# One weight gradient computed transposed and turned later, in a one-core forward-and-backward transformer block

## The chip, the core and the metric

The kernel runs on one core of one Trainium2 chip. The core has TensorE (PE; its weight loads are listed as PEld), VectorE (DVE), ScalarE (ACT), GpSimd (POOL), SyncE (SP) and 16 DMA engines. The metric is the device time of one execution in microseconds: the median of repeated runs. A change is judged by the ratio of its median to the one before.

## The reference

One transformer block, forward and backward, S = 2048 tokens of D = 640, in bfloat16. The outputs are the block's result and the gradients of six inputs, among them the three weights of the gated MLP (F = 1728).

```python
h  = x + A(layernorm(x), wqkv, wo)          # linear attention, 32 heads of 20
h2 = h + B(layernorm(h), w1, w3, w2)        # gated MLP

def B(x, w1, w3, w2):                       # x: [2048, 640]
    gate = x @ w1                           # [2048, 1728]
    up   = x @ w3
    hh   = silu(gate) * up
    return hh @ w2                          # w2: [1728, 640]

out, vjp = jax.vjp(f, A_x, A_wqkv, A_wo, B_w1, B_w3, B_w2)
grads = vjp(grad_out)                       # w2's gradient: hh.T @ grad_out, [1728, 640]
```

## The kernel before

The kernel is written as one stream of instructions by hand: the order in the source is the order in each engine's queue, and a queue stands still while its first instruction waits. Tokens are cut into 16 tiles of 128 rows. Data that a later stage needs in another layout is stored to DRAM and loaded back, often through a transposing DMA (`dmaT`, always issued on SP except for a few on ACT). `dma` issues on SP, `A.dma_start` on ACT, `dmaG` on POOL.

The stages, in order of time:

1. Norm and projections (0 to about 75 us). `load_x` brings in tiles of x, `stat` and `p1_norm` normalize them (on ACT for even tiles past 8, else on DVE), a table `v_steps` says beside which tile each of these is issued (steps marked "A" come ahead of the q activations of that tile, "B" behind), `trickle` says behind which tile a weight is loaded, and `outs` where results are stored. Tiles 8 and up are transposed by DMA (L250). `m_part` and `kvT_block` form the products for linear attention.
2. The MLP's forward pass and the first half of its backward pass (about 75 to 340 us), in four chunks of 512 tokens and 14 blocks of 128 columns of F (`mlp`). `mlp_ghh` computes one block of grad_out @ w2.T some calls ahead of its use (`AHEAD` = 2; 8 blocks are done before the loop). The side work of a chunk prepares the next chunk's tiles: `f2_at`, then `f2_hn` (normalize and store hn), then `f2_ht` (transpose it, by DMA for tiles 4 and up). `r_steps` says behind which block loads and stores of the attention's r are issued. `o2_steps` makes the output product with w2 of the chunk before, whose rows are loaded in four pieces in the first chunk.
3. w2's gradient (L1097; 340.5 to 399.4 us). `load_hh` brings hh from DRAM, transposed, in blocks of 512 columns (`blk`) with the first block in two halves. For each of 13 blocks of 128 rows of the gradient, two groups of 16 products run over the token tiles, with hh as the stationary operand and 320 columns of grad_out as the moving one. ACT copies the two banks (L1100) and issues the store to `out_6`. The last 64 rows go through `gw2_tail` (L1083): pairs of products, each on half of the array. Between the blocks SP is given the next loads: the last block of hh, the transposed w1 and w3 (`load_w13`), and the first two pieces of the gate's gradients (`load_gg`).
4. Gradients through the MLP's input and the attention (399.4 to 699.5 us): `ghn` (L1142), `gr`, then products of the attention, `dkv`, `gxn` (L1515).
5. The gradients of w1 and w3 (L1346; 699.5 to 816.2 us): seven blocks of up to 496 columns, five jobs of 16 products in each. `load_block(i + 2)` is issued when block i is done, since `gb` has two buffers. Each job's result is copied by ACT and stored from ACT's queue.

The core of stage 3:

```python
for j in range(2):
    for t in range(ST):
        T.matmul(acc[:, j, 0:HD], lhsT=hb[b][:, t, i * P:(i + 1) * P], rhs=g2[:, t, j * HD:(j + 1) * HD], ...)
A.copy(out=ob[:].rearrange("p (j n) -> p j n", j=2), in_=acc[:, :, 0:HD])
A.dma_start(out=out_6[fc * P:(fc + 1) * P, :], in_=ob[:])
```

Of the kernel before, what the change touches and what calls it, by code (L numbers as in the profile page):

```python
# [9 lines left out]
P = 128  # L10
# [15 lines left out]
NG = 27  # L26
# [29 lines left out]
def kernel(  # L56
# [39 lines left out]
    w_d = dram.tile([D, D], BF16, name="w_d")  # L96
    kvT_d = dram.tile([D, D], BF16, name="kvT_d")
    dwoT_d = dram.tile([D, D], BF16, name="dwoT_d")
    hn_d = dram.tile([S, D], BF16, name="hn_d")
    hh_d = dram.tile([F, S], BF16, name="hh_d")  # L100
    gg_d = dram.tile([2 * F, S], BF16, name="gg_d")
# [80 lines left out]
    def load_wq(a, b):  # L182
        dma(out=wqkv[:, :, a * HD:b * HD], in_=wq_v[:, :, a * HD:b * HD])

    def load_x(a, b):
        dma(out=x_sb[:, a:b, :], in_=xS[:, a:b, :])
# [133 lines left out]
    def q_tile(t):  # L320
        q_home(t)
        phi(p1_mm(t, 0), pqs[t], t)
# [101 lines left out]
    def m_part(m, tiles, js=(0, 1)):  # L424
        if m not in macc:
            macc[m] = [ps.tile([P, 512], F32, name="macc", tag=("m", "tr")[m % 2], bufs=2) for _ in range(2)]
        for t, j in [(t, j) for t in tiles for j in js]:
            n = HD + (m < 2) * j
            T.matmul(macc[m][j][:, 0:n], lhsT=pk_all[:, t, m * P:(m + 1) * P],  # L429
                     rhs=x_ext[:, t, j * HD:j * HD + n], start=(t == 0), stop=(t == ST - 1))  # L430
# [12 lines left out]
    def kvT_block(m, acc):  # L443

        a, b = M_H[m]
        n = (b - a) * DH
        for c in range(DT):
            T.matmul(acc[:, 0:n], lhsT=wqkv[:, c, 2 * D + m * P:2 * D + (m + 1) * P],
                     rhs=mT[:, c, a * DH:b * DH], start=(c == 0), stop=(c == DT - 1))
        masked(bd, acc[:, 0:n], m)  # L450
# [7 lines left out]
    zero_pads()  # L458
    load_w2T(0, 2 * P)
    load_g2T(0)  # L460
    load_x(8, 12)
    load_w2T(2 * P, 4 * P)
    load_wq(0, 2)
    load_x(12, ST)
    def warm_up(n, warm):
        for _ in range(n):
            T.matmul(warm[:, 0:P], lhsT=ones[:], rhs=ones[:], start=True, stop=True, skip_group_check=True)
# [34 lines left out]
    def load_wo():  # L502
        dma(out=wo[:], in_=A_wo.rearrange("(c p) n -> p c n", p=P))

    trickle = {4: w13[0], 5: w13[1], 9: lambda: load_wq(4, 6), 12: w13[2], 14: w13[3]}

    R = None
    v_steps = {1: (R, ("N", 4)), 2: (("S", 5), R, ("N", 5)), 3: (("S", 6), R, ("N", 6), ("C", 0)),
               4: (("S", 7), R, ("N", 7), ("S", 8)), 5: (R, ("N", 8), ("S", 9)), 6: (R, ("N", 9), ("S", 10)),
               7: (("S", 11), R, R, ("A", 10), ("L", 11)), 8: (("S", 12), R, R, ("S", 13)),  # L510
               9: (("N", 13), R, ("S", 14), ("B", 12)), 10: (R, R, ("S", 15)), 11: (R, ("B", 14), ("L", 15))}
    V_OPS = {"S": stat, "N": p1_norm, "C": p1_scale}

    def xn_out(g, q):
# [4 lines left out]
        sl = slice(g * TPC, (g + 1) * TPC)  # L519
        dma(out=pk_v[:, sl, :], in_=pk_all[:, sl, :])  # L520

    outs = {7: ((xn_out, 0, dma),), 8: ((group_out, 0),), 12: ((group_out, 1), (xn_out, 1, dma)), 13: ((group_out, 2),)}

    QT = (6, 7, 9, 11)
    M0 = {7: (0, 1, 2), 8: (3, 4, 5)}
# [47 lines left out]
    def big():  # L573
        return ps.tile([P, 2, 512], F32, name="bigx", tag="big", bufs=2)[:, 0]
# [49 lines left out]
    r_prod(5)  # L624
    m_part(4, range(5))
    q_tile(8)
    kvT_block(1, big())
    r_row(4)
    r_prod(6)
    phi_rest()  # L630
    m_part(4, range(5, 11))
    q_tile(9)
    phi_rest()
    for j in range(2):
# [110 lines left out]
    def f2_hn(t):  # L745
        hn[t] = (pf.tile([P, D], BF16, name="hn", tag="pql", bufs=4) if t == 2 else
                 pf.tile([P, D], BF16, name="hn", tag="h2", bufs=2) if t == 3 else
                 pf.tile([P, D], BF16, name="hn") if t % 2 else w2[:, FT, :])
        ln2.norm(hn[t][:], x_sb[:, t, :], t)
        if t < 2:  # L750
            f2_ht(t)
        for n in ((), (0, 1))[t] if t < 2 else (t,):
            dma(out=hn_v[:, n, :], in_=hn[n][:])
# [23 lines left out]
    def mlp_ghh(n):  # L777
        if n < SC * FT:
            ghh_chunk(n, lambda: ps.tile([P, W], F32, name="mm", bufs=4))
# [3 lines left out]
    def mlp(c, fc, between):  # L783

        k, i = divmod(fc, 2)
        n = c * FT + fc
        if n >= FILL - AHEAD:
            mlp_ghh(n + AHEAD)
        gp = mm5(w1, fc, hnT[c])
        if i == 0:  # L790
            pair[k] = [ew(name) for name in NAMES]
        sig, s2, gate, up = pair[k]
        A.activation(sig[:, i, :], gp[:], AF.Sigmoid)  # L793
        A.activation(s2[:, i, :], gp[:], AF.Sigmoid, scale=-1.0)
        drain(1)
        between()
        drain(1)
        if fc < FT - 1:
            upp = mm5(w3, fc, hnT[c])
            A.copy(out=up[:, i, :], in_=upp[:])  # L800
        else:
            V.memset(up[FL:, i, :], 0.0)
            A.copy(out=up[:FL, i, :], in_=gp[FL:])
        A.copy(out=gate[:, i, :], in_=gp[:])  # L804
        if i == 1:
            mlp_pair(c, k, *pair.pop(k), ghh.pop(n // 2))
# [152 lines left out]
    def sides(c):  # L959
        side = ({}, {})  # L960
        for i in range(TPC):
            k0 = 3 * i - (i == TPC - 1) * (1 + (c == 1)) + (-2, 1, 0)[c]
            for k, pos, f in ((k0 + 2, 1, f2_at), (k0 + 3, 0, f2_hn), (k0 + 3, 1, f2_ht)):
                if c == 0 and f is f2_at:
                    if i == 0:
                        continue
                    f = f2_at0
                if k0 == -2 and f in (f2_at0, f2_hn, f2_ht):
                    k, pos = (k + 1, 0) if f is f2_at0 else (k + 1, pos)
                if k >= 0:  # L970
                    side[pos].setdefault(k, []).append((f, i))
        return side
# [8 lines left out]
    def r_end(t):  # L981
        r_scale(t)
        r_out(t)

    r_steps = [{0: ((load_x, 6, 8),), 1: ((r4_out, 0, 2),), 2: ((r_load, 8),), 3: ((load_w2T, 10 * P, F),), 4: ((r_load, 9), (r4_out, 2, 4)),
                5: ((r_store, 7, 8),),
                10: ((xn_out, 2, dmaG),), 12: ((r_load, 10),)},
               {0: ((r_den, 8), (load_x, 8, 12)), 1: ((r_end, 8), (r_load, 11), (xn_out, 3, dmaG)), 2: ((r_den, 9),), 3: ((r_end, 9), (r_load, 12)),
# [4 lines left out]
    for c in range(SC):  # L993
# [3 lines left out]

        def run_side(pos, fc):
            if c + 1 < SC:
                for f, i in sorted(sides[c][pos].get(fc, ()), key=lambda x: (x[0] is f2_ht, x[1])):  # L1000
                    f((c + 1) * TPC + i)

        for fc in range(FT):
# [34 lines left out]
    drain(1)  # L1038


    hb, blk = {}, [(0, 512), (512, 512), (1024, 512), (1536, 192)]

    def load_hh(b):
        f0, fw = blk[b]
        hb[b] = U2.tile([P, ST, 512], BF16, name="hb", tag="ABCA"[b])
        for a, n in ((0, 2 * P), (2 * P, 2 * P)) if b == 0 else ((0, fw),):
            dmaT(out=hb[b][:, :, a:a + n], in_=hh_d[f0 + a:f0 + a + n, :])

    load_hh(0)
    for _ in o2_steps(SC - 1, A.dma_start):  # L1050
# [21 lines left out]
    def load_gg(j, c0, c1, q=dma):  # L1072
        if c0 == 0:
            ggb[j] = ba.tile([P, NG, 2 * P], BF16, name="ggb", bufs=2)
        q(out=ggb[j][:, c0:c1, :],
            in_=gg_d[c0 * P:c1 * P, j * 2 * P:(j + 1) * 2 * P].rearrange("(c p) w -> p c w", p=P))

    def gw2_tail():

        gt = ps.tile([P, 2, 512], F32, name="gt", tag="gw", bufs=4)  # L1080
        for t in range(ST):
            for j in range(2):
                T.matmul(gt[j * FL:(j + 1) * FL, 0, 0:HD], lhsT=hb[3][:, t, P:P + FL],  # L1083
                         rhs=g2[:, t, j * HD:(j + 1) * HD], start=(t == 0), stop=(t == ST - 1))
        ob = br.tile([P, HD], BF16, name="gts")
        A.copy(out=ob[:], in_=gt[:, 0, 0:HD])
        for j in range(2):
            A.dma_start(out=out_6[F - FL:F, j * HD:(j + 1) * HD], in_=ob[j * FL:(j + 1) * FL, :])

    for fc in range(FT - 1):  # L1090
        b, i = divmod(fc, 4)
        if fc == FT - 2:
            gw2_tail()
        acc = ps.tile([P, 2, 512], F32, name="gw", bufs=4)
        for j in range(2):
            for t in range(ST):
                T.matmul(acc[:, j, 0:HD], lhsT=hb[b][:, t, i * P:(i + 1) * P], rhs=g2[:, t, j * HD:(j + 1) * HD],  # L1097
                         start=(t == 0), stop=(t == ST - 1))
        ob = br.tile([P, D], BF16, name="gw2o", bufs=2)
        A.copy(out=ob[:].rearrange("p (j n) -> p j n", j=2), in_=acc[:, :, 0:HD])  # L1100
        A.dma_start(out=out_6[fc * P:(fc + 1) * P, :], in_=ob[:])
        if fc == 3:
            load_hh(3)
        if fc == 5:
            load_w13()
        if fc == 8:
            load_gg(0, 0, NG)
        if fc == 11:
            load_gg(1, 0, NG)
    ps.release()  # L1110
    U2.release()

# [437 lines left out]
    njob = 8  # L1550
    dmaT(out=g_h[:, 0:DT, :], in_=dwoT_d[:, :])
    dma(out=out3S, in_=g_h[:, 0:DT, :])
    for i, (f0, f1) in enumerate(blocks):
        n = f1 - f0
        for m in range(DT):
            last = (i, m) == (len(blocks) - 1, DT - 1)
            for a, b in ((0, n - P), (n - P, n)) if last else ((0, n),):
                c = (a + b) // 2
                halves = ((a, c), (c, b)) if i * DT + m < 5 else ((a, b),)
                out = [(x + y - a, z + y - a, to) for y, w in halves for x, z, to in both_grads(m, f0 + y, f0 + w)]  # L1560
                grad_job(hnN, m, lambda t: gb[i][:, t, a:b], b - a, out, A.dma_start)
        load_block(i + 2)
    ps.release()
    ex.release()
    bv.release()
# [33 lines left out]
```

## Time and profile before

| what | us |
|---|---|
| median of 3 runs | 822.12 (821.39 to 822.13) |
| profiled execution | 820.91 |
| span of its trace, first to last instruction | 819.1 |
| PE busy | 814.1 (5420 matmuls) |
| DVE busy | 452.4 |
| ACT busy | 323.6 |
| POOL busy | 130.9 |

By stretch of the span (us), with the busy time of three engines and the mean busy share of the DMA engines, which can pass 1 since packets in flight overlap:

| stretch | PE | DVE | ACT | DMA |
|---|---|---|---|---|
| 0 to 100 | 98.1 | 80.6 | 68.9 | 0.90 |
| 100 to 340.5 | 240.4 | 192.2 | 150.1 | 0.74 |
| 340.5 to 399.4 (w2's gradient) | 58.9 | 0.5 | 8.7 | 1.19 |
| 399.4 to 544.7 | 145.3 | 98.5 | 29.6 | 0.64 |
| 544.7 to 625.6 | 80.9 | 42.2 | 17.1 | 0.91 |
| 625.6 to 699.5 | 73.9 | 35.7 | 27.4 | 0.84 |
| 699.5 to 819.1 (w1's and w3's gradients) | 116.6 | 2.7 | 21.7 | 0.65 |

The granted clock of PE is 1.00 in all of them. All times are of one profiled execution; times on the span's clock start at its first instruction. Matmuls are pipelined, so the listed duration of one (299 ns at 320 columns) is longer than the distance from one to the next.

### The profile page before, as it was taken

The numbers are of one execution on the slowest core, as the hardware profiler recorded it, in microseconds if no ns is written. First come the engines' busy times: TensorE is split into PE (matmuls) and PEld (weight loads), VectorE is DVE, ScalarE is ACT, GpSimd is POOL, SyncE is SP. The second block draws the span as 40 slices with busy tenths as digits, with TensorE's granted clock in tenths as the row PEclk, the third lists the DMA queues.
The fourth block names the chain that finished last, engine by engine and source line by source line (L and its number), as shares of the span: only waits on it lengthen the run. The fifth ranks groups of instructions, "written<-read, shape, count | busy, mean of one in ns | idle before, by whom it ended". The sixth has DMA issues, their size and how long they took to land.

```text
span 819.1 us, 13944 instructions
## 1 busy us (share of the span) xinstructions
PE 814.1 (99%) x5420; PEld 512.8 (63%) x5420; DVE 452.4 (55%) x973; ACT 323.6 (40%) x603; POOL 130.9 (16%) x193
## 2 busy tenths in 40 slices
PE   9999999999999999999999999999999999999998
PEld 6677544555555555777777777777777777544444
DVE  7859987998898566300057777772781544200000
ACT  7856688665565666011122212222212334211111
POOL 2233333333222212100001111110220000000000
PEclk9999999999999999999999999999999999999999
DMA  9899699796485556999977877259974997967751
GB/s 264 219 290 239 166 244 327 225 245 173 127 211 156 169 170 167 222 261 226 257 176 180 211 197 200 58 107 187 287 195 93 181 194 159 239 164 186 160 141 36
DMA packets 323873, 157.88 MB, mean 193 GB/s; under 512 B 242784, under 2 KB 317056, under 8 KB 323808
## 3 DMA queue, kind: packets, MB, share of 16 engines
q1 hardware_dynamic: 281040, 116.18, 61.6%
q0 software_dynamic: 7328, 24.48, 8.7%
q10 hardware_dynamic: 35440, 16.34, 7.7%
q8 instruction: 42, 0.69, 0.4%
q14 instruction: 23, 0.19, 0.1%
HBM read 47.09 MB, written 51.13 MB: 120 GB/s over the span
## 4 chain that ended last, share of the span: by engine, by line
PE 96%; DVE 2%; ACT 1%; issue 0%; DMA 0%; POOL 0%; ACTq 0%; DVEq 0%
PE mm L394 20%; PE job L1346 20%; PE ghn L1142 14%; PE gxn L1515 8%; PE gw L1097 7%; PE o L910 4%; PE o L856 3%; PE gwo L1230 3%; PE big L267 3%; PE gr L1199 3%; PE dkv L1452 3%; PE macc L429 2%; PE at L654 2%; PE mm L267 1%; PE dkv L1380 1%; DVE st L147 1%
## 5 line engine op out<-in xcount | busy, mean ns | idle before, releaser
L1346 PE MATMUL job<-gb,hnN 128*128 128x496 bf16 (+3 forms) x576 | 116.8, 366 | 0.0
L1142 PEld LDWEIGHTS <-ggb 128*128 128x128 bf16 x864 | 84.5, 98 | 32.8
L1346 PEld LDWEIGHTS <-hnN 128*128 128x128 bf16 x576 | 55.8, 98 | 61.0
L394 PE MATMUL mm<-pqT,w 128*128 128x512 bf16 x405 | 93.8, 379 | 0.1
L394 PEld LDWEIGHTS <-w 128*128 128x128 bf16 x540 | 52.5, 98 | 63.4 <-issue 1.4
L1350 ACT CAST obs<-job 128x496 bf16<-128x496 f32 (+4 forms) x56 | 28.5, 510 | 123.7 <-PE job L1346 120.9
L1142 PE MATMUL ghn<-w13a,ggb 128*128 128x320 bf16 x448 | 63.5, 299 | 0.0
L1157 DVE SCALAR_TENSOR_TENSOR wb<-gs,hnb 128x640 f32<-128x640 bf16 x16 | 13.2, 825 | 88.7 <-ACT gs L1154 88.7
L1142 PE MATMUL ghn<-w13b,ggb 128*128 128x320 bf16 x416 | 61.4, 299 | 0.0
L394 PE MATMUL mm<-g2T,w2T 128*128 128x512 bf16 x240 | 59.6, 379 | 0.0
L1097 PE MATMUL gw<-g,hb 128*128 128x320 bf16 x416 | 56.8, 299 | 0.0
L1207 POOL TENSOR_TENSOR sz<-Zb,g_h 128x640 f32<-128x640 bf16 x16 | 20.2, 1261 | 197.7 <-DVE g_h L1208 197.7
L1097 PEld LDWEIGHTS <-hb 128*128 128x128 bf16 x416 | 40.6, 98 | 16.0 <-issue 0.3
L419 ACT CAST ghh<-mm 128x512 bf16<-128x512 f32 x48 | 28.3, 589 | 47.7 <-PE mm L394 40.1
L793 ACT ACTIVATE sig<-mm 128x512 bf16<-128x512 f32 x56 | 33.9, 605 | 26.4 <-PE mm L394 21.1
L1154 ACT ACTIVATE gs<-ghn 128x640 bf16<-128x640 f32 x16 | 11.3, 704 | 78.8 <-PE ghn L1142 73.9
L394 PEld LDWEIGHTS <-w2T 128*128 128x128 bf16 x260 | 25.4, 98 | 23.4
L267 PEld LDWEIGHTS <-pqT 128*128 128x128 bf16 x320 | 30.7, 98 | 13.7 <-ACT pqT L259 1.5
L267 PE MATMUL big<-wqkv,pqT 128*128 128x320 bf16 x250 | 38.6, 299 | 0.6 <-ACT pqT L259 0.3
L1346 PEld LDWEIGHTS <-g 128*128 128x128 bf16 x320 | 31.0, 98 | 11.5
L829 DVE TENSOR_TENSOR gate<-gate,sig 128x1024 bf16<-128x1024 bf16 x28 | 19.3, 689 | 33.2 <-ACT gate L804 30.5
L910 PE MATMUL o<-w,hhT 128*128 128x320 bf16 x224 | 35.0, 299 | 0.0
(219 smaller groups left out, 1369.9 us busy)
## 6 DMA issues: line engine op xcount, KB each, us to landing
hh_d<-hhT SPq DMA_DIRECT2D x24, 256.0 KB, 2.7
gg_d<-gate POOLq DMA_DIRECT2D x24, 256.0 KB, 4.3
gg_d<-ghh POOLq DMA_DIRECT2D x24, 256.0 KB, 3.4
ggb<-gg_d SPq DMA_DIRECT2D x6, 896.0 KB, 5.4
ggb<-gg_d ACTq DMA_DIRECT2D x6, 832.0 KB, 5.7
ggb<-gg_d SPq DMA_DIRECT2D x2, 1728.0 KB, 12.7
x_sb<-in_A_x_dram SPq DMA_DIRECT2D x5, 640.0 KB, 5.9
pk_d<-pk_all SPq DMA_DIRECT2D x4, 640.0 KB, 6.6
```

The source lines that it names most:

```text
L267: T.matmul(acc, lhsT=pqT[:, c, t * P:(t + 1) * P], rhs=wqkv[:, c, n0:n0 + HD], start=(c == 0), stop=(c == DT - 1))
L394: T.matmul(acc[:], lhsT=w[:, c, fc * P:(fc + 1) * P], rhs=rhs[:, c, :], start=(c == 0), stop=(c == DT - 1))
L419: A.copy(out=ghh[n // 2][:, n % 2, :], in_=acc[:])
L793: A.activation(sig[:, i, :], gp[:], AF.Sigmoid)
L856: T.matmul(accs[i, j][:, 0:HD], lhsT=hhT[c][:, fc, i * P:(i + 1) * P], rhs=w2[:, fc, j * HD:(j + 1) * HD], start=(first and fc == 0), stop ...
L910: T.matmul(o2["ps"][:, 0:HD], lhsT=hhT[c][:, fc, i * P:(i + 1) * P], rhs=w2[:, fc, j * HD:(j + 1) * HD], start=(fc == 0), stop=(fc == FT - 1))
L1097: T.matmul(acc[:, j, 0:HD], lhsT=hb[b][:, t, i * P:(i + 1) * P], rhs=g2[:, t, j * HD:(j + 1) * HD], start=(t == 0), stop=(t == ST - 1))
L1142: T.matmul(acc[:, j, 0:HD], lhsT=ggb[t // 2][:, k, lo:lo + P], rhs=rhs[:, j * HD:(j + 1) * HD], start=(k == 0), stop=(k == NG - 1))
L1199: T.matmul(gr[t][:, j, 0:HD], lhsT=ghT[t][:, c, :], rhs=wT2[:, c, j * HD:(j + 1) * HD], start=(c == 0), stop=(c == DT - 1))
L1346: T.matmul(acc[:, 0:n], lhsT=lhs[:, t, m * P:(m + 1) * P], rhs=rhs(t), start=(t == 0), stop=(t == ST - 1))
L1350: A.copy(out=ob, in_=acc[:, 0:n])
L1515: T.matmul(acc[:, j, 0:HD], lhsT=g, rhs=wqT[:, k, j * HD:(j + 1) * HD], start=(k == 0), stop=(k == 14))
```

## The change

Stage 3 computes the gradient's transpose: grad_out is now the stationary operand (five blocks of 128 columns) and hh the moving one, in four blocks of 256, 448, 512 and 512 columns. That gives 20 pieces of 16 products, each into one PSUM bank of one of two sets of four (`gw0`, `gw1`). Each piece is copied by ACT and stored, as it is, to a new DRAM tile `gw2T_d`; pieces of 448 columns are padded to 512 by a POOL memset. In stage 5, SP loads the four blocks back through the transposing DMA into free parts of `g_h` (`gw2_turn`), one behind each of the first four blocks, and stores each one block later to `out_6` (`gw2_out`). The tail function is gone. `load_hh` makes one transfer a block, and the loads between the pieces are issued at other places in the loop.

The rest changes orders. In stage 1, x tiles 10 and 11 are loaded with 12 to 15 instead of with 8 and 9, half of w3 and a store of pk are issued behind later tiles, tile 14 is normalized ahead of q's activations, and the second `kvT_block` comes behind a part of `m_part`. In stage 2, `f2_ht` is called in `f2_hn`, ahead of the store of hn, for tiles 4 and up, two transfers in `r_steps` change places, and `mlp_ghh` skips one call at the start of the second chunk and then runs one block ahead instead of two. In stage 5, eight jobs instead of five store in two parts.

```diff
+    gw2T_d = dram.tile([D, 4 * 512], BF16, name="gw2T_d")
...
-    load_x(8, 12)
+    load_x(8, 10)
     load_w2T(2 * P, 4 * P)
     load_wq(0, 2)
-    load_x(12, ST)
+    load_x(10, ST)
...
-    trickle = {4: w13[0], 5: w13[1], 9: lambda: load_wq(4, 6), 12: w13[2], 14: w13[3]}
+    trickle = {4: w13[0], 7: w13[1], 9: lambda: load_wq(4, 6), 12: w13[2], 14: w13[3]}
...
-               9: (("N", 13), R, ("S", 14), ("B", 12)), 10: (R, R, ("S", 15)), 11: (R, ("B", 14), ("L", 15))}
+               9: (("N", 13), R, ("S", 14), ("B", 12)), 10: (R, R, ("S", 15)), 11: (R, ("A", 14), ("L", 15))}
...
-    outs = {7: ((xn_out, 0, dma),), 8: ((group_out, 0),), ...
+    outs = {7: ((xn_out, 0, dma),), 9: ((group_out, 0),), ...
...
     q_tile(8)
-    kvT_block(1, big())
...
     m_part(4, range(5, 11))
+    kvT_block(1, big())
     q_tile(9)
...
         ln2.norm(hn[t][:], x_sb[:, t, :], t)
-        if t < 2:
+        if t < 2 or t >= TPC:
             f2_ht(t)
...
-        if n >= FILL - AHEAD:
-            mlp_ghh(n + AHEAD)
+        if FILL - AHEAD <= n < FT or n > FT:
+            mlp_ghh(n + (AHEAD if n < FT else 1))
...
-            for k, pos, f in ((k0 + 2, 1, f2_at), (k0 + 3, 0, f2_hn), (k0 + 3, 1, f2_ht)):
+            for k, pos, f in ((k0 + 2, 1, f2_at), (k0 + 3, 0, f2_hn)):
...
-    r_steps = [{..., 2: ((r_load, 8),), 3: ((load_w2T, 10 * P, F),), ...
+    r_steps = [{..., 2: ((load_w2T, 10 * P, F),), 3: ((r_load, 8),), ...
...
-    hb, blk = {}, [(0, 512), (512, 512), (1024, 512), (1536, 192)]
+    hb, blk = {}, [(0, 256), (256, 448), (704, 512), (1216, 512)]
...
-        for a, n in ((0, 2 * P), (2 * P, 2 * P)) if b == 0 else ((0, fw),):
-            dmaT(out=hb[b][:, :, a:a + n], in_=hh_d[f0 + a:f0 + a + n, :])
+        dmaT(out=hb[b][:, :, 0:fw], in_=hh_d[f0:f0 + fw, :])
...
+    for n in range(len(blk) * DT):
+        b, m = divmod(n, DT)
+        f0, fw = blk[b]
+        tag = "gw0" if n // 4 in (0, 2) or n in (16, 17) else "gw1"
+        acc = ps.tile([P, 512], F32, name="gw", tag=tag, bufs=4)
         for t in range(ST):
+            T.matmul(acc[:, 0:fw], lhsT=g2[:, t, m * P:(m + 1) * P], rhs=hb[b][:, t, 0:fw], start=(t == 0),
+                     stop=(t == ST - 1))
+        ob, fp = br.tile([P, 512], BF16, name="gw2o", bufs=3), (fw + P - 1) // P * P
+        if fp > fw:
+            G.memset(ob[:, fw:fp], 0.0)
+        A.copy(out=ob[:, 0:fw], in_=acc[:, 0:fw])
+        A.dma_start(out=gw2T_d[m * P:(m + 1) * P, b * 512:b * 512 + fp], in_=ob[:, 0:fp])
+        if n == 4:
             load_hh(3)
+        if n == 9:
             load_w13()
+        if n in (12, 15):
+            load_gg((n - 12) // 3, 0, NG)
...
+    turned = [DT, DT + 2, DT + 6, 0]
+
+    def gw2_turn(b):
+        n = (blk[b][1] + P - 1) // P
+        dmaT(out=g_h[:, turned[b]:turned[b] + n, :], in_=gw2T_d[:, b * 512:b * 512 + n * P])
+
+    def gw2_out(b):
+        f0, fw = blk[b]
+        n, k = fw // P, turned[b]
+        dma(out=out_6[f0:f0 + n * P, :].rearrange("(k p) d -> p k d", p=P), in_=g_h[:, k:k + n, :])
+        if fw % P:
+            dma(out=out_6[f0 + n * P:f0 + fw, :], in_=g_h[0:fw % P, k + n, :])
+
     for i, (f0, f1) in enumerate(blocks):
...
-                halves = ((a, c), (c, b)) if i * DT + m < 5 else ((a, b),)
+                halves = ((a, c), (c, b)) if i * DT + m < 8 else ((a, b),)
...
         load_block(i + 2)
+        if 0 < i <= 4:
+            gw2_out(i - 1)
+        if i < 4:
+            gw2_turn(i)
```

More of the change, by code (lines that the diff above doesn't have):

```diff
@@ L520, in group_out @@
         dma(out=pk_v[:, sl, :], in_=pk_all[:, sl, :])
-    outs = {7: ((xn_out, 0, dma),), 8: ((group_out, 0),), 12: ((group_out, 1), (xn_out, 1, dma)), 13: ((group_out, 2),)}
+    outs = {7: ((xn_out, 0, dma),), 9: ((group_out, 0),), 12: ((group_out, 1), (xn_out, 1, dma)), 13: ((group_out, 2),)}
     QT = (6, 7, 9, 11)
@@ L967, in sides @@
                     f = f2_at0
-                if k0 == -2 and f in (f2_at0, f2_hn, f2_ht):
+                if k0 == -2 and f in (f2_at0, f2_hn):
                     k, pos = (k + 1, 0) if f is f2_at0 else (k + 1, pos)
@@ L983, in r_end @@
         r_out(t)
-    r_steps = [{0: ((load_x, 6, 8),), 1: ((r4_out, 0, 2),), 2: ((r_load, 8),), 3: ((load_w2T, 10 * P, F),), 4: ((r_load, 9), (r4_out, 2, 4)),
+    r_steps = [{0: ((load_x, 6, 8),), 1: ((r4_out, 0, 2),), 2: ((load_w2T, 10 * P, F),), 3: ((r_load, 8),), 4: ((r_load, 9), (r4_out, 2, 4)),
                 5: ((r_store, 7, 8),),
@@ L999, in run_side @@
             if c + 1 < SC:
-                for f, i in sorted(sides[c][pos].get(fc, ()), key=lambda x: (x[0] is f2_ht, x[1])):
+                for f, i in sorted(sides[c][pos].get(fc, ()), key=lambda x: x[1]):
                     f((c + 1) * TPC + i)
@@ L1076, in load_gg @@
             in_=gg_d[c0 * P:c1 * P, j * 2 * P:(j + 1) * 2 * P].rearrange("(c p) w -> p c w", p=P))
-    def gw2_tail():
-        gt = ps.tile([P, 2, 512], F32, name="gt", tag="gw", bufs=4)
-        for t in range(ST):
[L1082 to L1102, printed above, removed]
+    for n in range(len(blk) * DT):
[3 more added lines that the diff above has]
+        acc = ps.tile([P, 512], F32, name="gw", tag=tag, bufs=4)
+        for t in range(ST):
+            T.matmul(acc[:, 0:fw], lhsT=g2[:, t, m * P:(m + 1) * P], rhs=hb[b][:, t, 0:fw], start=(t == 0),
[6 more added lines that the diff above has]
+        if n == 4:
             load_hh(3)
-        if fc == 5:
+        if n == 9:
             load_w13()
[L1106 to L1109, printed above, removed]
+        if n in (12, 15):
+            load_gg((n - 12) // 3, 0, NG)
     ps.release()
```

## The prediction

> **What bounds the kernel now.** I read the page first: the share of each engine, and the chain that ended last.
>
> ```profile
> span 819.1 us, 13944 instructions
> ...
> PE   9999999999999999999999999999999999999998
> ...
> PE 96%; DVE 2%; ACT 1%; issue 0%; DMA 0%; POOL 0%; ACTq 0%; DVEq 0%
> ```
>
> TensorE is busy in every slice and is 96% of the chain. Since its matmul ends are modelled, I looked next for real gaps, in TensorE's waits:
>
> ```profile
> PE warm L467 <- DVE zero L124: 1.1, 1, 1.1
> PE big L267 <- ACT pqT L259: 0.3, 1, 0.3
> ```
>
> 1.4 us in all. From the starts of successive matmuls I find some 3 us of stalls, nearly all before 15 us or between 95 and 103 us; one of 0.28 us stands at 37.7 us. The rest runs at streaming pace, so an edit can win only by taking columns or matmuls from TensorE, and can lose by making it wait. Third, the chain in order of time around the edited stage (start, length, what):
>
> ```profile
> 333.37 7.17 PE o L856 x52
> 340.54 52.16 PE gw L1097 x384
> 392.70 2.29 PE gt L1083 x32
> 394.99 4.45 PE gw L1097 x32
> 399.44 19.56 PE ghn L1142 x144
> ```
>
> The stage has no gap at either end and takes 399.44 - 340.54 = 58.90 us. Fourth, SP's queue in the same stretch (start, time that the issues hold SP):
>
> ```profile
> 329.51 34.37 SPq L1047 DMA_TRANSPOSE hb<-hh_d  x5
> 363.94 9.75 SPq L1066 DMA_TRANSPOSE w13a<-in_B_w_dram  x1
> 373.91 12.30 SPq L1067 DMA_TRANSPOSE w13b<-in_B_w_dram  x1
> 386.27 1.27 SPq L1068 DMA_TRANSPOSE w13a<-w13tail  x1
> 387.84 4.77 SPq L1075 DMA_DIRECT2D ggb<-gg_d  x2
> ```
>
> SP issues back to back: the stream goes at the pace at which data moves, and the windows give the stage a DMA share of 1.19. Its landings are the deadlines here. Fifth, a block of the last stage, by windows (stretch, TensorE busy and count first, DMA share and GB/s last), with its load in SP's queue and among the DMA issues (last: us to landing):
>
> ```profile
> 733.00:749.70 16.70, 16.70 (x81) 7.83 (x80) 0.00 (x0) 2.86 (x5) 0.00 (x0) 1.00 0.67 161
> ```
>
> ```profile
> 716.26 8.01 SPq L1492 DMA_TRANSPOSE gb<-gg_d  x1
> ```
>
> ```profile
> gb<-gg_d SPq DMA_TRANSPOSE x1, 10.9
> ```
>
> The load holds SP for 8.0 us and lands after 10.9 (10.6 to 12.5 over the five loads that wait for a block), in a block of 16.73 us.
>
> **TensorE's sum.** Lengths of the chain give the price of a matmul: 52.16/384 = 135.8 ns at 320 columns, and the piece "PE mm L394 x35" of 7.55 us gives 215.7 at 512. So 0.416 ns a column and 2.6 ns each. Narrow ones keep to it: 20 matmuls of 140 columns and 5 of 160 (gkvT, L1399) took 1.56 us, and the line gives 1.56, though a weight load is listed at 98 ns. Hence 189.1 ns at 448 columns and 109.2 at 256.
> - Removed: the whole 58.90 us. The 416 full matmuls are 56.5 of it; the 32 of the tail, two at a time on half the array, cost 2.29, and switching to them some 0.1.
> - Added: 80 x 109.2 + 80 x 189.1 + 160 x 215.7 ns = 8.74 + 15.13 + 34.51 = 58.38 us.
> - Net: -0.52 us. The columns are the same (1728 x 5 x 16 = 138,240, the tail's pairs counted once); 112 fewer issues at 2.6 ns, a pair counted once, are 0.29 us, and the stalls of 0.09 into the tail and 0.16 out of it nearly all the rest. The width of 256 is not in the trace for a full array: its upper bound is 135.8, the 320 row, which would add 2.1 us; I take the line, since rows on both sides of 256 lie on it.
>
> **Inputs of the stage.** The first piece of hh, 256 columns, is issued as before (329.51, landed 339.47) and needed at 340.54. The second is now 448 columns and needed when the first five products end, at 340.54 + 8.74 = 349.28. In the trace 512 columns had landed at 344.8 and 1024 at 353.8; 704 lie 192/512 of the way, at 348.2. Bounds: 17.5 ns a column (the 512 after that) gives 347.3, 20.8 (the 256 before) 348.8. Cover 0.5 to 2.0 us; beyond it a late microsecond costs one. The third piece comes near 357.5 for 364.4, the fourth waits for block 0 (349.3, before SP reaches it) and is needed at 381.7. w1, w3 and the two gg loads keep their order and bytes; the first gg load landed at 397.05 and is needed at 398.92: cover 1.87 us.
>
> **Copies and stores.** 20 ACT copies of at most 0.59 us (the 512-column row) replace 14; ACT is busy 8.7 us of 58.9. A copy now waits for the landing of the store three pieces earlier (three buffers; stores took 3.5 to 9.3 us), and only later copies and stores queue behind it. TensorE has eight banks before it meets this, 12 us and more. By their tags, the last two pieces lie in banks that the next stage's first two accumulators don't use, so those wait for pieces ended 7 us before. POOL's five memsets have an idle engine. Cost: nothing.
>
> **The last stage.** Behind each of four loads, SP now gets a store of a turned piece and the turning of the next. The nearest rows: turning dwoT (640 x 640) held SP 4.4 us and landed after 7.1; its store landed after 3.7. For 512 columns, 3.5 us of SP and at most 7.1 to land. SP is then free 8.0 + 0.4 + 3.5 = 12 us after a block's end (13.3 behind the slowest load), before the next at 16.73. The store waits for a turning one block old; what queues behind that is the next turning and the next load. The load itself is ahead of both, so its cover of 4.2 us or more stays. Splitting three more stores in two: ACT issues of 0.44 us on an idle engine. The final store doesn't change.
>
> **The moved steps.** `mlp_ghh` skips one call, so from there up to its last full chunk everything else on TensorE comes one chunk (1.08 us) earlier. That is order, not work, but two loads of w2 lose cover: its row blocks 6 to 9 landed at 142.12 and would be read at 142.8 instead of 143.9; the last block landed at 146.31, read at 147.0 instead of 148.1. Cover 0.7 us each; if gone, one for one. The transposes of hn go ahead of hn's stores, and in the first stage x tiles 10 and 11, half of w3 and a store of pk go behind transposes: SP work, TensorE doesn't wait there now, and the moved transposes land earlier. The 0.28 us stall at 37.7 us comes from ACT reading an accumulator after DVE waited for POOL; nothing touches that. Moving the second kvT product behind 12 matmuls and the normalization of tile 14 ahead of q's activations (0.94 us of ACT; the accumulator is then read by 42.1 for a matmul at 42.4): nothing.
>
> [...] In the stretch from 330 to 400 us ACT's queue had 2246 packets taking 10.9% of 16 engines, 54 ns each. The change writes the gradient in 20 x 128 = 2560 rows instead of 1792. By bytes the stream loses only the padding, 82 KB at 250 GB/s, 0.3 us, within the cover of 1.87. By packets it could lose 768 x 54 / 16 = 2.6 us up to the gg load, which then comes 0.7 us late. [...] The trace's packet times overlap (the shares sum to over 100%), so 54 ns is more than a packet's own cost, and I take the bytes.
>
> **Sum.** The profiled execution is 820.91 us (span 819.1, 1.8 around it), so 820.4 after. The median of the runs is 822.12, 1.2 above it; the same difference gives 821.6.
>
> **Rivals.**
> - *The stage's SP stream comes late* (slower). One mechanism: stores in more, smaller packets delay the transposes and loads queued on SP. It decides where the 448 columns land after 349.28 or the gg load after 398.92. By the packet count -0.52 + 0.7 = +0.2: 822.3. Slower than the measurement can tell needs 2.2 us of lateness, 4 us of delay. For: the stage's DMA share of 1.19. Against: same bytes, same order. Chance 0.14, half of it below a visible loss.
> - *Turned pieces hold up the blocks' loads* (slower). If the turning's full 7.1 us came in front of the slowest load, 12.5, it would land at 19.6, 2.9 us late, for each of three loads: +8.6 - 0.5 = +8.1, 830.2. For: both use one queue. Against: the order, load first. 0.04.
> - *Matmuls of 256 columns cost as much as 320* (slower): +2.1 - 0.5 = +1.6: 823.7. Against: the 140- and 160-column rows. 0.02.
> - *Stalls go as well* (faster): the 0.28 at 37.7, or more of the 3 us: 821.3, and faster than can be told only if over 1.1 of the 3 us went with the 0.5. 0.08, half of it that far.
> - *The w2 rows come late*: up to 0.7 us, 822.3. 0.08.
> - *The forecast, -0.5*: 0.64.
>
> **How the numbers follow.** About 0.2%, 1.6 us, is what a measurement of this kernel can tell from no change. Slower by more: 0.07 of the first rival, the second's 0.04 and half the third, together 0.12, and 0.02 for several small delays at once: 0.14. Faster by more: 0.04. Within: 0.82. Low end: the forecast less 0.28 and the 0.65 by which the runs spread below their median and a little: 820.7. High end: 821.6 plus the packet bound's 0.7 and w2's 0.7 and some spread: 823.2.
>
> **What would show it.** Right: the chain's gw pieces last 58.4 us with no gap before them or before ghn, loads of the last stage still land within 12.5 us, TensorE's last matmul ends 0.5 earlier. Wrong: a wait of gw's matmuls on hb, of ghn on ggb, of o on w2 or of job on gb; or a 256-column piece of 16 matmuls far from 1.75 us.

## The result, and the profile after

The changed kernel takes 826.83 us (median of 6 runs, 825.53 to 829.36) against 821.77 for the kernel before beside it: a ratio of 1.006, with a 95% interval of 1.0041 to 1.0080. The prediction was 821.6, within 820.7 to 823.2. The profiled execution of the changed kernel is 827.78 us, its span 826.1; before, 820.91 and 819.1. So the two spans lie 7.0 us apart, 2 more than the medians (5.1): the profiled execution of the changed kernel was one of its slower ones.

First the page: its span, TensorE's row of the 40 slices, and the shares of the chain.

```profile
span 826.1 us, 13695 instructions
...
PE   8998999999999999999999999999999999999998
...
PE 86%; DVE 10%; DMA 1%; ACT 1%; issue 1%; POOL 0%; DVEq 0%; ACTq 0%
```

The fourth slice, 62 to 83 us, is no longer full (nor is the first), and the chain now runs over DVE for 10% of its length instead of 2%, nearly all of it ahead of w2's gradient. TensorE's waits (total, times, longest) name what it waited for:

```profile
PE big L268 <- DMA pqT<-x_sb: 2.6, 2, 2.0
PE trm L718 <- DVE bd L212: 2.3, 1, 2.3
PE warm L468 <- DVE zero L125: 1.1, 1, 1.1
PE mm L395 <- ACT up L801: 1.0, 1, 1.0
```

Only the third was there before. Next the stages that hold the new gradient, from the chain in order of time (start, length, what):

```profile
341.12 7.17 PE o L857 x52
348.29 24.08 PE gw L1084 x161
...
404.80 1.89 PE gw L1084 x8
406.69 15.35 PE ghn L1129 x113
...
706.74 116.65 PE job L1333 x576
```

The gradient takes 406.69 - 348.29 = 58.40 us, and no gap stands before it or behind it. The last stage takes 116.65 us, as before. Its loads still come early, six of them with a median of 10.3 us:

```profile
gb<-gg_d SPq DMA_TRANSPOSE x6, 10.3
g_h<-gw2T_d SPq DMA_TRANSPOSE x4, 6.1
```

The loss lies in the first 110 us. The time from one matmul's start to the next, less the usual time for its width, gives the stalls. Behind the first 15 us the larger ones are, in the profile after, 0.76 us at 39.7, 2.21 at 44.9, 2.48 at 76.4 and 1.12 at 108.6 (before: 0.28 at 37.7 and 0.28 at 102.0), a further 0.3 near 197, and 1.7 us for a stretch of 3.41 us in which TensorE ran at half clock. That sums to 8.0 us more, and less 0.5 for the gradient to 7.5, against the 7.0 between the spans. I take the large ones in turn.

**At 76.4 us.** DVE's queue after (start, time, operation), and TensorE behind it:

```profile
75.15 0.86 DVE L374 TENSOR_REDUCE rden<-pr 128x16 f32<-128x320 f32 x2
...
76.96 0.97 DVE L381 TENSOR_TENSOR pql<-pql,rden 128x640 bf16<-128x640 bf16 x1
...
78.67 0.30 DVE L212 TENSOR_TENSOR bd<-bigx,mask 128x140 bf16<-128x140 f32 x1
```

```profile
79.02 0.44 PE L718 MATMUL trm<-ident,hx 128*128 128x128 bf16 x5 [2.32 <-DVE bd L212]
```

Before:

```profile
72.56 0.29 DVE L211 TENSOR_TENSOR bd<-bigx,mask 128x140 bf16<-128x140 f32 x1
```

```profile
73.94 0.51 PE L717 MATMUL trm<-ident,hx 128*128 128x128 bf16 x5
```

`bd<-bigx` is the masked copy by which `kvT_block(1)` empties its PSUM bank, one of the banks in which TensorE's results lie, and `trm`, in the pool opened next, takes that memory. Before, the copy was done 1.1 us before `trm` began. Now its matmuls come 12 later on TensorE, and its copy stands behind `r_row(4)` (75.15 to 77.9) and a `phi_rest` on DVE, and TensorE waits for all of them: 3.5 us of DVE work, less the 1.1 us there were to spare, is 2.4.

**At 39.7 and 44.9 us.** SP's queue after, 32 to 45 us (start, time that the issue holds SP):

```profile
32.73 0.51 SPq L233 DMA_DIRECT2D w<-in_B_w_dram  x1
35.42 2.53 SPq L251 DMA_TRANSPOSE pqT<-x_sb  x2
37.99 0.58 SPq L521 DMA_DIRECT2D pk_d<-pk_all  x1
38.62 0.51 SPq L184 DMA_DIRECT2D wqkv<-in_A_wqkv_dram  x1
40.51 3.55 SPq L251 DMA_TRANSPOSE pqT<-x_sb  x2
```

Before, the same two transfers and the transposes of tiles 14 and 15 stood at:

```profile
24.65 0.57 SPq L232 DMA_DIRECT2D w<-in_B_w_dram  x1
33.22 0.51 SPq L520 DMA_DIRECT2D pk_d<-pk_all  x1
```

```profile
41.79 2.52 SPq L250 DMA_TRANSPOSE pqT<-x_sb  x2
```

The half of w3 (832 KB) now stands just ahead of the transposes of tiles 12 to 15, and the store of pk (640 KB), with wq's load (800 KB), just ahead of those of tiles 14 and 15. By the trace the half lands at 38.87, wq's load at 46.49, and the transposes right behind them at 40.04 (tile 12) and 47.15 (tile 14, 6.6 us after its issue). Before, tile 14's was issued 1.3 us later and landed at 44.36, after 2.6 us.

**Half clock.** By windows (stretch, TensorE busy and count first, granted clock, DMA share and GB/s last), with bounds from the trace's clock records:

```profile
76.97:80.38 3.41, 1.36 (x13) 1.06 (x13) 2.62 (x6) 0.88 (x2) 0.27 (x1) 1.00 0.89 188
80.38:83.80 3.42, 3.42 (x23) 2.71 (x21) 1.35 (x5) 1.80 (x6) 0.00 (x0) 0.50 0.66 238
```

For 3.41 us after the wait, TensorE is busy throughout but at clock 0.50. In four of the six runs the mean clock of the span was below 1.000 (0.996 to 0.998); the two at 1.000 took 825.5 and 825.6 us, and the three at 0.998 from 826.6 to 827.8.

### The profile page after: what moved, and what is told of

It reads as the page before. It is cut to its first block, busy times and chain, and to the rows that moved or that the text cites. A ratio compares the mean times of both kernels' runs of the same rounds, so it can differ in the third digit from the quotient of the medians.

```text
span 826.1 us, 13695 instructions
## 1 busy us (share of the span) xinstructions
PE 813.4 (98%) x5260; PEld 502.0 (61%) x5292; DVE 452.8 (55%) x973; ACT 324.6 (39%) x609; POOL 131.4 (16%) x198
## 4 chain that ended last, share of the span: by engine, by line
PE 86%; DVE 10%; DMA 1%; ACT 1%; issue 1%; POOL 0%; DVEq 0%; ACTq 0%
PE job L1333 19%; PE mm L395 15%; PE ghn L1129 14%; PE gxn L1502 8%; PE gw L1084 7%; PE o L857 3%; PE gwo L1217 3%; PE gr L1186 3%; PE dkv L1439 3%; PE o L911 2%; PE big L268 2%; PE at L655 2%; DVE st L148 2%; DVE s L830 1%; PE macc L430 1%; PE mm L268 1%
## 5 line engine op out<-in xcount | busy, mean ns | idle before, releaser
L1084 PE MATMUL gw<-hb,g 128*128 128x512 bf16 (+2 forms) x316 | 58.4, 345 | 0.2
L1084 PEld LDWEIGHTS <-g 128*128 128x128 bf16 x320 | 31.3, 98 | 27.0
L1333 PEld LDWEIGHTS <-g 128*128 128x128 bf16 x320 | 31.0, 98 | 11.6
L1089 ACT CAST gw2o<-gw 128x512 bf16<-128x512 f32 (+2 forms) x20 | 10.4, 518 | 65.4 <-PE gw L1084 22.0
```

Source lines behind the costliest of these rows:

```text
L1084: T.matmul(acc[:, 0:fw], lhsT=g2[:, t, m * P:(m + 1) * P], rhs=hb[b][:, t, 0:fw], start=(t == 0), stop=(t == ST - 1))
L1333: T.matmul(acc[:, 0:n], lhsT=lhs[:, t, m * P:(m + 1) * P], rhs=rhs(t), start=(t == 0), stop=(t == ST - 1))
```

## The experiments

Each kernel was compared with the kernel before on the same chip. "e1" and so on are short names.

| kernel | median us | ratio to before, 95% interval | runs with clock 0.998 or less |
|---|---|---|---|
| the change | 826.83 | 1.0060, 1.0041 to 1.0080 | 4 of 6 |
| e1: kvT product back | 822.91 | 1.0011, 1.0003 to 1.0020 | 0 of 11 |
| e2: first stage's transfers back | 823.90 | 1.0026, 1.0016 to 1.0037 | 3 of 8 |
| e3: both back | 821.08 | 0.9994, 0.9984 to 1.0004 | 0 of 11 |
| e4: w2's gradient alone | 821.61 | 1.0001, 0.9992 to 1.0010 | 0 of 11 |
| t2: shorter wait | 824.10 | 1.0023, 1.0013 to 1.0032 | 0 of 9 |
| t1: longer wait | 829.54 | 1.0091, 1.0076 to 1.0106 | 4 of 4 |
| f1: e1, half of w3 back too | 821.71 | 0.9993, 0.9984 to 1.0002 | 0 of 11 |
| f2: e1, store of pk back too | 824.22 | 1.0022, 1.0012 to 1.0032 | 4 of 8 |
| c1: e1, half of w3 late | 822.59 | 1.0008, 0.9999 to 1.0016 | 0 of 11 |
| c2: e3, half of w3 late, pq store early | 824.29 | 1.0029, 1.0016 to 1.0043 | 1 of 6 |
| f3: e3, half of w3 at 89 us | 822.15 | 0.9997, 0.9988 to 1.0005 | 0 of 11 |
| f4: e3, half of w3 on ACT | 821.64 | 0.9996, 0.9987 to 1.0005 | 0 of 11 |

### Undoing the parts

e1, against the change:

```diff
+    kvT_block(1, big())
     r_row(4)
     r_prod(6)
     phi_rest()
     m_part(4, range(5, 11))
-    kvT_block(1, big())
```

> The changed kernel with the second kvT product back at its old place, ahead of r_row(4) on DVE's queue; nothing else differs. Theory 1 (the wait of 2.3 us of the trm transposes on DVE's bd, and the 3.4 us at half clock that follow it, come from this move alone): that wait goes, the clock stays at 1.0, and with 2.5 us of the wait and 1.7 us of the half clock gone the time falls from 826.8 to 822.6 us (2.5 alone: 824.3, if the half clock has another cause). Theory 2 (a chain of DVE and SP work behind it is what is late, and the wait only moves on): the wait at 76 us goes but another of 1.5 to 2.5 us stands before 110 us, and the time stays above 825.5. The waits of 0.8 and 2.2 us at 40 and 45 us stay in both.

822.91 us, 3.9 below the change; every run at clock 1.000, and `trm` no longer waits. Theory 1 holds, with the time 0.3 above its 822.6. In the stretch from 20 to 100 us one group of waits is left, with the two at 40 and 45 us (0.81 and 1.85):

```profile
PE big L268 <- DMA pqT<-x_sb: 2.3, 2, 1.7
```

e2, against the change:

```diff
-    load_x(8, 10)
+    load_x(8, 12)
...
-    load_x(10, ST)
+    load_x(12, ST)
...
-    trickle = {4: w13[0], 7: w13[1], ...
+    trickle = {4: w13[0], 5: w13[1], ...
...
-               ... 11: (R, ("A", 14), ("L", 15))}
+               ... 11: (R, ("B", 14), ("L", 15))}
...
-    outs = {..., 9: ((group_out, 0),), ...
+    outs = {..., 8: ((group_out, 0),), ...
```

> The changed kernel with the first stage's transfers and norms in the old order: x tiles 10 and 11 loaded with 8 and 9, half of w3 behind tile 5, the store of pk behind tile 8, tile 14 normalized behind q's activations; the kvT product stays at its new place. Theory 1 (bulk transfers now stand ahead of the transposes of tiles 12 and 14 on SP): the waits at 40 and 45 us go, 0.5 + 2.2 = 2.7 us less, 824.1 us; the trm wait of 2.3 us and, in most executions, the half clock behind it stay. Theory 2 (the two waits are absorbed by the trm wait later, because DVE is the one that is late there): the trm wait grows by what is saved, and the time stays within 0.5 us of 826.8.

823.90 us, 2.9 below the change, as theory 1 has it. The waits at 40 and 45 us are gone and the one of `trm` is as long as it was, so neither hides the other. One that was not expected came up, 1.4 us at 31 us: tile 9's transpose behind the half of w3. The profile of before doesn't have it; e3's and e4's, with the same order there, have 1.5 and 1.2. In before, tile 9's transpose landed 0.8 us after the half of w3; in these three, 2.0 us after it. Why is not shown. Three runs at clock 0.998 took 825.1 to 825.6, five at 1.000 took 822.8 to 823.9: medians 825.31 and 823.64, a difference of 1.7 us, which is half of the 3.41 us at half clock.

e3 takes both edits together.

> Both of the two other edits together: kvT and the first stage's transfers in the old order, the later orders and w2's transposed gradient as in the changed kernel. Theory 1 (these moves are the whole loss but for the 0.8 us wait of mm on ACT's up at 108 us): 826.8 - 2.7 - 4.2 = 819.9 to 821.3 us, against 821.8 before; TensorE has no wait over 0.4 us before 100 us. Theory 2 (the transposed gradient, its stores or its turning cost time that the trace does not show as a wait): 823 us or more though the waits are gone.

821.08 us: 5.8 below the change, against 3.9 + 2.9 = 6.8 from the two alone, a difference that the intervals allow. The gradient is transposed here and, within the interval, nothing is lost. Theory 1 missed one thing: it expected no wait over 0.4 us before 100 us, and the trace has the one of 1.5 at 31 us, and another of 1.55 at 7 us. That trace is of one of the slower executions (822.50).

e4 is the kernel before with the new stage, the new DRAM tile and `gw2_turn` and `gw2_out` of the last stage; all orders are those of before.

> The kernel before with w2's gradient alone changed: transposed pieces in two sets of banks, stored to DRAM and turned in the last stage; every other order as before (and five split jobs in the last stage, as before). Theory 1 (the prediction's sum for the stage holds): 58.4 us in the stage instead of 58.9, no new wait, 0.5 us faster: 821.3 against 821.8. Theory 2 (the new gradient itself brings a loss, in the transfers it adds): 823 us or more.

821.61 against 821.97, the ratio 1.0001 with 1 well inside its interval. In its trace the stage takes 401.50 - 343.10 = 58.40 us, like the change's. So the stage is 0.50 us shorter than before, as summed, and the whole is no different by this measurement. A gain of 0.5 us is not shown in the time, and a loss of over 0.8 us is outside its interval. "No new wait" does not hold for its trace, which is of the slowest of the 11 executions (822.79): besides the 1.2 us at 31 us it has 1.4 us at 133 us, for an ACT copy, and neither is in the trace of before, though up to there the two kernels issue the same work in the same order. Its gradient starts at 343.10 us, against 340.54. So one trace can differ from another by some 2 us without any edit ahead of that point, and small waits are better judged by the medians.

### The wait by its place in DVE's queue, and the clock

t2, against the change:

```diff
     r_row(4)
     r_prod(6)
-    phi_rest()
     m_part(4, range(5, 11))
     kvT_block(1, big())
+    phi_rest()
```

> The changed kernel with the second kvT product issued ahead of phi_rest instead of behind it: TensorE's order is that of the changed kernel, only DVE gets the product's masked copy 0.9 us earlier, still behind r_row(4). Theory 1 (the trm transposes wait for the place of that copy in DVE's queue): the wait falls by 0.9 us, from 2.5 to about 1.6 us, and no execution has the 3.4 us at half clock, since too little idle time is left for it: 826.8 less 0.9 and 1.7, 824.2 us; the clock is 1.000 in all runs. Theory 2 (the half clock does not depend on the wait, or comes from any wait at this place): still about half of the runs at a clock of 0.998, median above 825.

t1, against the change; `r_head(5)` later on becomes `r_T(5)`:

```diff
     m_part(4, range(5, 11))
+    r_row(5)
     kvT_block(1, big())
```

> The changed kernel with r_row(5), 2.7 us of DVE, moved from later on to just ahead of the second kvT product, so that the product's masked copy stands 2.7 us further back in DVE's queue. Theory 1 (wait by the place in the queue; half clock when a stretch of 3.4 us holds enough idle time): the wait of TensorE at 76 us becomes 5.2 us, and every run now has a stretch at half clock, 0.998 or lower in all of them: 826.8 + 2.7 = 829.5 us, and 829 to 830. Theory 2 (the half clock is chance): two of three runs as before at 0.998, the others at 1.000.

t2: 824.10, the wait 1.65 us. t1: 829.54, the wait 5.17. In both, time and wait are within 0.1 us of theory 1: TensorE's wait grew and shrank one for one with the DVE work ahead of the masked copy (2.48 us in the change, 1.65 with 0.9 us of that work less, 5.17 with 2.7 us more). (For t2's time that may be partly luck: in t2's trace the waits at 40 and 45 us, which its edit does not touch, are 1.12 and 0.52 us, against 0.76 and 2.21 in the change's.) The clock went with it: none of 9 runs below 1.000 in t2, all 4 in t1. By the clock records of t1, two stretches of 3.41 us are at half clock, back to back:

```profile
76.27:79.68 3.41, 0.64 (x5) 0.33 (x4) 3.24 (x7) 0.59 (x2) 1.42 (x3) 1.00 1.01 211
79.68:83.09 3.41, 1.17 (x8) 0.93 (x8) 2.81 (x7) 0.45 (x1) 1.29 (x2) 0.50 0.81 282
83.09:86.50 3.41, 3.41 (x21) 2.46 (x19) 0.33 (x1) 2.42 (x7) 0.00 (x0) 0.50 0.00 0
```

and t2, with the wait in the first line, has none:

```profile
73.01:76.43 3.42, 2.32 (x18) 1.56 (x16) 3.32 (x6) 1.95 (x4) 1.70 (x3) 1.00 1.13 196
76.43:79.84 3.41, 3.02 (x34) 2.52 (x34) 2.63 (x10) 2.54 (x7) 0.00 (x0) 1.00 0.87 228
```

### Which transfer

f1 and f2 are e1 with one more edit undone: `5: w13[1]` in f1, `8: ((group_out, 0),)` in f2.

> The changed kernel with the second kvT product at its old place and the half of w3 behind tile 5 again; x tiles 10 and 11, the store of pk and tile 14's norm as in the changed kernel. Theory 1 (the half of w3 is the transfer that tips the balance, since in SP's queue 3.5 us of it stand ahead of tiles 12 to 15): the wait at 40 us goes and the one at 45 us falls from 1.9 to about 1.1, as with that half loaded late; tile 9's transpose now lands behind the half, so a wait of 1 us or more may come at 31 us instead: 822.9 - 0.8 - 0.8 + 1 = 822.3 us. Theory 2 (the store of pk, two tiles later than before, is what holds tile 14): the 1.9 us at 45 us stay, and the time is 822.9 or more.

> The changed kernel with the second kvT product at its old place and the store of pk behind tile 8 again, ahead of the transposes of tiles 12 and 13 instead of behind them; the half of w3 stays behind tile 7. Theory 1 (bytes ahead in the queue, whatever they are): the store of 655 KB is 2.7 us, now ahead of tile 12 as well; the wait at 40 us grows from 0.8 to 2 us or more, and the one at 45 us shrinks by about as much: 822 to 823.5 us, no gain. Theory 2 (the store is the cause of the wait at 45 us): that wait goes and nothing comes in its place, 821 us.

f1: 821.71 us, 1.2 below e1, and their intervals do not meet; no wait at 31 or 40 us, and 0.96 at 44. f2: 824.22, 1.3 above e1, though the two intervals meet: the wait at 45 us goes, and 2.76 us stand at 40 instead, with the half clock behind them in four of eight runs. Those four have a median of 824.37, the others of 823.59. So here the half clock made 0.8 us and not 1.7. Tile 14's transpose landed at 45.37, at the end of the slow stretch, and a faster TensorE may have had to wait for it; that is not shown.

```profile
PE big L268 <- DMA pqT<-x_sb: 2.6, 1, 2.6
```

So the half of w3 tips it. By their ratios to before, f1 (0.9993) gains all that e3 (0.9994) does, so the other moves of the first stage, the loads of x tiles 10 and 11, the store of pk and tile 14's norm, cost nothing that can be told once the half is back. Moving the store back while the half stays only shifts the wait: a load and a store alike held up the transposes issued behind them (behind the half of w3 alone, TensorE's wait at 40 us was 0.81 us in e1; behind the half and the store, 2.76 in f2).

c1 and c2 leave the half of w3 out of the first stage's middle. c2 also moves the pq store:

```diff
     ps.release()
     load_x(0, 6)
+    w13[1]()
```

```diff
-    (f2_half, 0, 1), (r_store, 4, 5), ... (f2_m_out,), (q_out, 10, 14),
+    (f2_half, 0, 1), (q_out, 10, 14), (r_store, 4, 5), ... (f2_m_out,),
```

> The changed kernel with the second kvT product at its old place, and the half of w3 that is loaded behind tile 7 loaded at the end of the first stage instead, behind x tiles 0 to 5. Theory 1 (transposes on SP land behind whatever bulk transfer was issued before them): the half is 852 KB, 3.5 us at the stage's pace, so the transposes of tiles 12 to 15 land that much earlier; the wait of 0.8 us at 40 us and the 1.9 us at 45 us both go, 822.9 - 2.7 = 820.2 us. Theory 2 (the wait at 45 us is made by the store of pk and wq(4,6) alone, issued 0.6 and 2.5 us ahead of tile 14's transpose): only the 0.8 us go and most of the 1.9 stays: 822 us.

> The changed kernel with the first stage and the kvT product in the old order, but the half of w3 that stood behind tile 5 loaded at the end of the stage, and the store of pq (q_out) issued on POOL ahead of two stores of r instead of behind them. Theory 1: the wait of 1.2 to 1.5 us of TensorE at 31 us (tile 9's transpose lands behind that half of w3) goes, and the wait of 0.5 us at 103 us (ACT's first sigmoid follows the landing of the pq store) too: 821.1 - 1.3 - 0.5 = 819.3 us, below both kernels. Theory 2 (the time is set elsewhere, or the half of w3 now comes late for its first product at 98 us): no gain, 821 us or more, with a wait of mm on w.

c1: 822.59, near theory 2. The wait at 40 us is gone and the one at 45 us falls from 1.85 to 1.11, no further, since the pk store and wq's load are still there; the median is only 0.3 below e1, within the intervals of both. c2 is a miss, 3.2 us above e3. From 20 to 80 us it has no wait over 0.35 us, but the two moves made new ones:

```profile
PE trh L767 <- DVE hn L161: 1.8, 1, 1.8
PE at L656 <- DMA Wp<-pkx: 1.3, 1, 1.3
```

Wp's transposes now land behind the half of w3 (issued at 77.23, landed at 85.33; the first of Wp's at 86.00). And the pq store, ahead of r's on POOL's queue, makes one r store land at 98.94; the normalization into the tile that it frees starts at 99.02, and `trh` waits for that.

f3 issues the half behind `r_head(5)` instead; f4 leaves it behind tile 5, on ACT's queue.

> First stage and kvT product in the old order, all else as in the changed kernel, but the half of w3 is loaded where SP's queue is free, behind the transposes of Wp and of r's tile 5 at about 89 us, instead of behind tile 5. Theory 1 (it is only in the way ahead of tile 9's transpose): no wait at 31 us, none at 86 or 97 us, the half lands near 93 us and is first read at 98.5; 821.1 - 1.3 = 819.8 us, below both kernels. Theory 2 (it comes late there, or delays hn's transposes as it delayed those of Wp): waits of mm on w or of trh near 98 us, 821 us or more.

> First stage and kvT product in the old order, all else as in the changed kernel, but the half of w3 behind tile 5 is issued from ACT's queue instead of SP's, at the same point of the program. Theory 1 (a transpose waits because it stands behind bulk bytes in the same queue): tile 9's transpose, 4.7 to 6.4 us from issue to landing behind the half, takes 2.4 to 3.5 us; no wait at 31 us; 821.1 - 1.3 + 0.5 for ACT at most, 819.8 to 820.3 us. Theory 2 (it is the DMA engines' bandwidth that is shared, whatever the queue): the transpose still takes 4.5 us or more, and the time stays at 821 us.

f3's profile has the waits that theory 1 forecast, though not its time: no wait over 0.55 us from 20 us on, span 819.1, time 820.84. But its 11 runs reach from there to 823.49 with a median of 822.15, and the other executions were not traced, so what differs in them stays open. f4: no wait at 31 us, median 821.64. A queue of its own did not shield the transposes, though, and in that theory 2 is right: issued on ACT at 21.15, the half landed at 28.11 and tile 8's transpose, issued on SP at 23.38, at 28.71, after 5.33 us (2.6 to 3.5 in the change, e1 and f1). ACT had issued the half some 3.5 us sooner than SP did in f1; tile 9's transpose landed at 29.28, in time. So f4's gain of the wait comes from the earlier issue, by this trace, and not from the other queue. That bandwidth is what the two shared is theory 2's reading and was not shown by itself. No version here beats the kernel before by more than its interval; the best ones tie with it, some 5 us below the change.

## Why the prediction was wrong

- **TensorE's sum: right.** 58.38 us predicted, 58.40 in the change, e3 and e4. The 256-column matmuls took 109 ns from start to start and the 448-column ones 189.
- **Inputs, copies, last stage: right.** No matmul of the stage, of `ghn` or of the last stage waits. By the trace the first hh transfer landed at 346.81 for 348.29, the second at 355.99 for 357.03 (cover 1.0, predicted 0.5 to 2.0), the first gg load at 402.42, over 4 us before `ghn` begins.
- **The packet count** did not come true. The first gg load landed 54.1 us after the stage's start, against 56.5 before; by the packet count it would have been 2.6 later. The loads are issued at other places of the loop than before (that of w1 21.2 us after the stage's start, against 23.4), so what the larger number of packets costs by itself is shown by no run. Nor does a run show the packet bound's 0.7 us in the high end of the range: the gg load landed over 4 us ahead of `ghn`, which did not wait.
- **The moved steps: this is the step that failed**, in three terms that were set at nothing or left out. (1) "Moving the second kvT product behind 12 matmuls ...: nothing" counted TensorE's order, and not that the product's masked copy moves past 3.5 us of DVE work (75.15 to 78.67), nor who needs its bank. The trace of before had the price: a copy done 1.1 us ahead of `trm`. Measured: a wait of 2.5 us, and 3.9 us of time with the clock (e1 against the change; 2.8, e3 against e2). (2) "SP work, TensorE doesn't wait there now, and the moved transposes land earlier" is wrong in its last part: tile 14's transpose was issued earlier and landed 2.8 us later, since the half of w3 and the store of pk had moved to just ahead of it. Measured 2.9 us (e2 against the change) or 1.8 (e3 against e1), of which the half of w3 alone makes 1.2 by the medians (f1 against e1) and, by the ratios to before, all. (3) The prediction had no term for a wait's second cost, the half clock: when it comes, 1.7 us behind the wait of `trm` (e2's runs), 0.8 behind the one at 40 us (f2's).
- **The later orders** (`mlp_ghh`, `f2_ht`, `r_steps`, the split stores) are in e3 and not in e4, and the two don't differ by more than their intervals. No `o` waited for w2.
- **The rivals**: those with a mechanism for a loss looked at the new stage, the last one or the w2 rows; none looked at the moves of the first stage. "Several small delays at once" had 0.02 and comes nearest, but two of the delays were over 2 us and one of them had a cause that could be read from the trace of before.

The wait at 108 us (1.1, before 0.3) is not from any move tested: in the traces of before, the change and all but one of the experiments, ACT's first sigmoid of the MLP starts 0.23 us after the pq store lands, and that store took 4.5 to 5.2 us. In c2, where it landed early, the sigmoid waited for something else. Why the store varies stays open.

## What to carry to other kernels

A step that is moved takes its last instruction along: look up which engine frees its buffer, what then stands ahead of it in that engine's queue, and who takes that memory next. For a load moved later, ask not only whether its own data come in time but which small transfer, due soon, is now issued behind its bytes, on the same queue (tile 14's transpose took 6.6 us to land, against 2.6 before) or, as in f4, on another (tile 8's took 5.33); in the trace of before, the time from that transfer's landing to its first use is what there is to spare. Where TensorE has no slack, a wait of 2.5 us cost up to 1.7 us more than its length here, through the clock (e2's runs at 0.998 against those at 1.000).

## What the hardware showed

The granted clock fell to 0.50 after waits of 2.5 us and more: 2.48 in the change, 5.17 in t1, 2.76 in f2. In the change's trace the record of half clock is 3.413 us long and begins 75.09 us after the start of the trace's first clock record, 22 times that length. Cut into such lengths from that start, the trace has one in which TensorE was busy for 1.36 us, and it was followed by half clock; in each of the other whole ones TensorE was busy for 2.3 us or more, and none of them was. In t1 the lengths ahead of the two at half clock had 0.64 and 1.17 us busy; in f2 the one ahead had 1.18:

```profile
38.83:42.24 3.41, 1.18 (x9) 0.61 (x7) 3.12 (x12) 2.81 (x5) 0.79 (x3) 1.00 1.23 254
42.24:45.65 3.41, 3.05 (x12) 1.79 (x13) 1.52 (x5) 0.16 (x1) 0.89 (x3) 0.50 1.14 327
```

In e2's trace the same wait of 2.5 us falls across two lengths, with 2.27 and 2.23 us busy, and the clock stays at 1.00:

```profile
72.92:76.33 3.41, 2.27 (x17) 1.50 (x16) 3.31 (x6) 1.95 (x4) 1.66 (x3) 1.00 1.00 146
76.33:79.75 3.42, 2.23 (x25) 1.85 (x25) 1.81 (x7) 1.76 (x5) 0.00 (x0) 1.00 1.10 199
```

So the same wait came with half clock in one trace and without it in another, and the two differ in how it falls on these lengths. That they run on by themselves, whatever the kernel does, is the author's reading of the change's trace and was not tested by a run.
